# q/k from natural positions, an earlier v and convolution, a gate column with a ScalarE gate, and band-mask rows beside the head rows in 14 of 24 attention steps

## The chip, the cores and the metric

One core of one Trainium2 chip. The metric is the device time of one execution in microseconds; lower is better. Before the change three runs gave 301.47, 302.58 and 312.01 us (median 302.58). On one core the runs of one kernel scatter by 2 to 7%: a run more than 1.5% above the fastest of its kernel is called slow, and its mean granted TensorE clock is usually lower. A ratio is the mean time of one kernel's fast runs over that of the other's fast runs of the same rounds, so it is not quite the ratio of the medians quoted beside it.

## The reference, cut to what matters

```python
x = A_q                                          # [1, 2048, 640], bf16
g = sigmoid((x * gate_w).sum(-1, keepdims=True)) # one gate value per position
a = x * (causal_fft_conv(shortconv(A_k) * A_v, ssm_k) + shortconv(A_k) * A_v * ssm_D)
# b: 32 heads of 20, every query sees 8 keys, 2 positions apart
q, k, v = split(x @ B_wqkv)
b = softmax(q . k[pos - 2*w] / sqrt(20), w = 0..7) . v @ B_wo
out = g * a + (1 - g) * b
```

Of the kernel before, what the change touches and what calls it, by code (L numbers as in the profile page):

```python
# [76 lines left out]
def attn_consts():  # L77
# [21 lines left out]
    return dict(mk=_np_bf16(mkz.reshape(128, -1)), mq=_np_bf16(mqz.reshape(128, -1)), valid=_np_bf16(valid), ident=_np_bf16(np.eye(128)))  # L99
# [35 lines left out]
def kernel(  # L135
# [37 lines left out]
    xTn = p0.tile([128, NDT, 2, XP], BF, name="xTn", tag="hT")  # L173
# [10 lines left out]
    xT = pC.tile([128, NDT, XW], BF, name="xT")  # L184
    Wp = pC.tile([128, NDT, 2, NDT, 4, 32], BF, name="Wp")
    WV = pC.tile([128, NDT, D], BF, name="WV")
    wg = pC.tile([128, NDT], BF, name="wg")
    valid = pC.tile([128, 18], BF, name="valid")
    sB = ExitStack()
    pB = sB.enter_context(tc.tile_pool(name="pB", bufs=1, side="left", reuse_waits="tile"))  # L190
    wl = pB.tile([128, 4, D], BF, name="wl")
    wraw = pB.tile([128, D, 4], BF, name="wraw")
    Wn = pB.tile([128, NDT, 2, D], BF, name="Wn", tag="Wn")
# [24 lines left out]
    for c in range(4):  # L218
        load_x(c)
    nc.sync.dma_start(WV[:], W3[:, :, 2, :])  # L220
    nc.vector.memset(xTn[:, :, :, 0:PRE], 0.0)
    nc.vector.memset(xTn[:, :, :, PRE + S // 2:XP], 0.0)
    nc.gpsimd.dma_start(wraw[:], raw(A_shift_k, 0, [[0, 128], [4, D], [1, 4]]))
    nc.gpsimd.dma_start(valid[:], ca["valid"].ap())
    nc.gpsimd.dma_start(wg[:], gate_w.rearrange("(t p) -> p t", p=128))
    load_kv(0)
# [14 lines left out]
    def kv_gen():  # L241
# [3 lines left out]
        for c in range(4):  # L245
# [9 lines left out]
            kvo = pB.tile([128, 4 * D], BF, name="kvo", tag="kvo", bufs=2)  # L255
# [14 lines left out]
    def transposes(j):  # L270
        tr = ppv.tile([128, 8, 128], BF, name="trx", tag="trx")
        for dt in range(NDT):
            nc.tensor.transpose(tr[:, dt, :], xN[:, j, 128 * dt:128 * dt + 128], ident[:, :])
        a = PRE + 128 * (j // 2)
        ld.copy(xTn[:, :, j % 2, a:a + 128], tr[:, 0:NDT], NDT * 128, eng="ad"[j % 2])

    def windows(e, g):
        n = 6
        s0 = xTn[:, :, e, QB * n * g:QB * n * g + QB * (n - 1) + KB]
        src = bass.AP(tensor=s0.tensor, offset=s0.offset, ap=[list(s0.ap[0]), list(s0.ap[1]), [QB, n], [1, KB]])  # L280
        c0 = (NSB * e + n * g) * KB
        nc.vector.tensor_copy(xT[:, :, c0:c0 + n * KB].rearrange("p t (b k) -> p t b k", k=KB), src)  # L282

    def vproj(m):
        ps = ppv.tile([128, 2, 512], F32, name="psv", tag="mm", bufs=3)
        for a in range(2):
            for dt in range(NDT):
                nc.tensor.matmul(ps[:, a, 0:320], lhsT=xT[:, dt, 128 * m:128 * m + 128], rhs=WV[:, dt, 320 * a:320 * a + 320],  # L288
                                 start=(dt == 0), stop=(dt == NDT - 1))
        nc.scalar.copy(VW[:, m, :, 0:DH].rearrange("p (a h) d -> p a h d", a=2),  # L290
                       ps[:, :, 0:320].rearrange("p a (h d) -> p a h d", h=16))

# [6 lines left out]
    def gate():  # L299
        grow = pB.tile([1, S], F32, name="grow", tag="Wn")  # L300
        for c in range(6):
            gps = ppv.tile([128, 512], F32, name="gps", tag="trx")
            for dt in range(NDT):
                rhs = xT[:, dt, 384 * c:384 * c + 384].rearrange("p (b c) -> p b c", c=KB)[:, :, PRE:KB]
                nc.tensor.matmul(gps[0:1, 0:6 * QB], lhsT=wg[:, dt:dt + 1], rhs=rhs,
                                 start=(dt == 0), stop=(dt == NDT - 1))
            p = 6 * QB * (c % 3)
            n = min(6 * QB, S // 2 - p)
            nc.scalar.activation(grow[:].rearrange("o (n two) -> o two n", two=2)[:, c // 3, p:p + n], gps[0:1, 0:n], ACT.Exp, scale=-1.0)
        nc.sync.dma_start(g_scr[:].unsqueeze(0), grow[:])  # L310
        for g in range(4):
            nc.sync.dma_start(g_nat[32 * g:32 * g + 32, :], raw(g_scr[:], 16 * g, [[64, 32], [1, 16]]))
# [12 lines left out]
    def permute_w():  # L325
        for w in range(2):
            nc.scalar.copy(Wp[:, :, w, :, :, 0:DH].rearrange("p a t h d -> p a (t h) d"),
                           Wn[:, :, w, 0:400].rearrange("p a (h d) -> p a h d", d=DH))
            yield
            nc.scalar.copy(Wp[:, :, w, :, :, DH:32].rearrange("p a t h d -> p a (t h) d"),  # L330
                           Wn[:, :, w, 400:D].rearrange("p a (h d) -> p a h d", d=32 - DH))
            yield

    QKP = ((1, KB, 0, 0), (0, QB, PRE, KB))

    def qk_part(ft, c, part, ps):
        which, wd, off, z = QKP[part]
        nb = 8 if c < 4 else 4
        for dt in range(NDT):
            rhs = xT[:, dt, 512 * c:512 * c + KB * nb].rearrange("p (b c) -> p b c", c=KB)[:, :, off:off + wd]  # L340
            nc.tensor.matmul(ps[:, 0:nb * wd], lhsT=Wp[:, dt, which, ft].rearrange("p h c -> p (h c)"), rhs=rhs,  # L341
                             start=(dt == 0), stop=(dt == NDT - 1))

    def qk_evac(ft, c, part, ps, eng):
        _, wd, _, z = QKP[part]
        nb = 8 if c < 4 else 4
        ld.copy(kq[ft // 4][:, ft % 4, 8 * c:8 * c + nb, z:z + wd], ps[:, 0:nb * wd].rearrange("p (b c) -> p b c", b=nb), nb * wd, eng=eng)
# [10 lines left out]

    def qk_gen(fts):
        for ft in fts:  # L360
            for c in range(5):
# [528 lines left out]
```

## The kernel before: what the change and the argument touch

Positions are split into even and odd; 36 windows of 64 keys and 57 queries cover them. The tiles `kq` hold k and q side by side, 4 heads per tile at partitions 32h. A head has 20 rows, so partitions 32h+20 to 32h+31 are free. The q/k projection fills them with pieces of the heads 20 to 31, and `send_rest` copies these pieces by DMA to their proper places in the second `kq` tile.

```python
def send_rest(ft):                     # SP queue, 28 copies in all
    ...
        nc.sync.dma_start(kq[1][dst:dst + n, t % 4, :, :],
                          kq[ft // 4][src:src + n, ft % 4, :, :])   # n partitions x 8712 B

def scores(i):                         # half an attention step: two heads
    gi, t, hf = halves[i]
    for hh in range(2):                # band mask: a matmul of 11 rows ahead of the scores
        r = 32 * (2 * hf + hh)
        nc.tensor.matmul(sc[:, hh, 0:NW], lhsT=mk[r:r + NF, :], rhs=mq[r:r + NF, :], start=True, stop=False, ...)
    ...                                # then 24 small score matmuls, 20 rows each, added to the mask
            nc.tensor.matmul(sc[...], lhsT=kqt[r:r + DH, t % 4, si, 0:KB],
                             rhs=kqt[r:r + DH, t % 4, si, KB:CB], start=False, stop=True, ...)
    nc.scalar.activation(ETs[i % NET][...], sc[...], ACT.Exp, scale=SCALE)

# main order: all transposes, windows of x (VectorE), v, gate, q/k of two feature tiles,
# rest of the convolution, load_hn(0), load_hn(1), send_rest(0), send_rest(1), then
# 24 attention steps with "units" of later work between their parts:
# steps 0-7 q/k of three tiles, 8-11 late v, from 12 on output projection and the first FFT
```

`load_hn` loads the long filter (512 KB each) which VectorE transposes during attention; both it and the copies use the one SP queue, whose timelines show the issues in program order, each behind the waits of those ahead of it. `b_scr` is a DRAM scratch that takes the attention output from the tile `fin`. `kv_scr`, `G`, `Hb` and `qg` belong to the FFT stages and the final product.

## Time and profile before

| Profiled run of before (fast, span 302.1 us, mean clock 0.932) | starts at, us |
|---|---|
| first v matmul | 20.27 |
| first q/k matmul | 46.35 |
| first attention score | 64.80 |
| first late v matmul (step 8) | 112.49 |
| first output projection (step 12) | 134.53 |
| first `s<-Am,G` matmul (FFT stage after attention) | 187.03 |
| first load of `qg` from the SP queue | 209.71 |
| last inverse stage | 280.75 |

I call these the milestones and read them off TensorE's and the queue's timelines. A change that gains in one stage shows as an earlier milestone. The views themselves are in the prediction.

### The profile page before, as it was taken

How to read it: one execution, taken by the hardware profiler on the slowest of the kernel's cores; microseconds unless marked ns; L12 is line 12 of the kernel's file. 1: busy time of each engine (PE TensorE's matmuls, PEld its weight loads, DVE VectorE, ACT ScalarE, POOL GpSimd, SP SyncE). 2: the span in 40 equal slices, each digit the busy share in tenths (PEclk: the TensorE clock that was granted, in tenths of full speed). 3: DMA queues.
4: the chain of work that ended last, by engine and by line, in shares of the span. 5: the costliest groups of instructions: out<-in, count | busy, mean ns of one | idle time of the engine just before them, and what ended most of it. 6: DMA issues, size and time to landing. Idle time of an engine off the chain costs nothing. (4 is left out here: it accounts for less than half of the span.)

```text
span 302.1 us, 12078 instructions
## 1 busy us (share of the span) xinstructions
PE 246.1 (81%) x5468; PEld 170.3 (56%) x5482; DVE 199.8 (66%) x304; ACT 175.6 (58%) x247; POOL 17.3 (6%) x36
## 2 busy tenths in 40 slices
PE   2569959999999996999889998997968789587530
PEld 1447624554545454556556665776867769577410
DVE  2169999995248686687346465319578597975692
ACT  2344864566434452354537564789587868976670
POOL 3820000000000000000000000000000000000042
PEclk9999989999999997799999999999797969997955
DMA  7999722023665515103664242274998762360075
GB/s 223 339 311 403 282 81 85 4 89 98 152 147 131 100 46 113 57 2 98 180 184 118 86 138 89 58 162 94 243 282 207 186 139 70 75 158 2 4 208 142
DMA packets 18842, 42.19 MB, mean 140 GB/s; under 512 B 3944, under 2 KB 11448, under 8 KB 17783
## 3 DMA queue, kind: packets, MB, share of 16 engines
q1 hardware_dynamic: 17800, 39.21, 46.5%
q0 software_dynamic: 992, 2.23, 2.9%
q8 instruction: 42, 0.69, 1.0%
q14 instruction: 8, 0.07, 0.1%
HBM read 26.22 MB, written 7.87 MB: 113 GB/s over the span
## 5 line engine op out<-in xcount | busy, mean ns | idle before, releaser
L341 PE MATMUL pj<-xT,Wp 128*128 128x456 bf16 (+3 forms) x236 | 50.7, 347 | 0.9 <-issue 0.3
L587 ACT ACTIVATE ET<-sc 128x684 bf16<-128x684 f32 x48 | 34.3, 740 | 18.1 <-PE sc L584 17.5
L122 ACT CAST kq<-pj 128x456 bf16<-128x456 f32 (+3 forms) x39 | 19.5, 528 | 26.7 <-PE pj L341 26.4
L341 PEld LDWEIGHTS <-Wp 128*128 128x128 bf16 x250 | 21.7, 97 | 18.1 <-issue 0.3
L452 PE MATMUL s<-Am,G 64*128 64x64 bf16 x1280 | 22.4, 190 | 9.6 <-issue 6.2
L485 DVE TENSOR_TENSOR Hb<-Up,Hb 128x1024 bf16<-128x1024 bf16 x40 | 25.3, 687 | 7.3 <-DMA Hb<-Hb 4.4
L498 PE MATMUL i<-M,Hb 128*128 128x128 bf16 x320 | 26.6, 249 | 4.1 <-DVE Hb L485 4.0
L122 ACT CAST Am<-s 128x1024 bf16<-128x1024 f32 x27 | 26.6, 1036 | 3.8 <-PE s L428 3.5
L498 PEld LDWEIGHTS <-Hb 128*128 128x128 bf16 x320 | 25.0, 153 | 6.1 <-DVE Hb L485 5.7
L452 PEld LDWEIGHTS <-G 64*128 64x128 bf16 x1280 | 20.0, 95 | 12.7 <-issue 8.8
L648 DVE CAST fin<-op 128x320 bf16<-128x320 f32 x24 | 11.7, 489 | 19.2 <-PE op L643 17.9
L643 PE MATMUL op<-wo,oT 128*128 128x320 bf16 x120 | 20.0, 300 | 4.1 <-ACT oT L630 2.7
L247 DVE TENSOR_TENSOR pr<-kvw,wl 128x2560 bf16<-128x2560 bf16 x16 | 22.8, 1487 | 0.1
L122 ACT CAST Hb<-s 128x1024 bf16<-128x1024 f32 x19 | 19.0, 1024 | 4.5 <-PE s L452 4.5
L606 PEld LDWEIGHTS <-ET 64*64 64x64 bf16 x1152 | 13.6, 110 | 13.3 <-issue 11.9
L517 DVE STREAM_TRANSPOSE hb<-hn 128x512 bf16<-128x512 bf16 x20 | 20.0, 1045 | 0.2
L616 DVE TENSOR_TENSOR oS<-O,rd 128x240 bf16<-128x240 f32 x48 | 17.3, 403 | 3.9 <-DMA kv_scr<-kvo 3.1
L584 PE MATMUL sc<-kq 20*64 20x57 bf16 x1152 | 18.4, 192 | 0.0
L606 PE MATMUL O<-VW,ET 64*64 64x21 bf16 x1152 | 18.0, 180 | 0.1
L288 PE MATMUL psv<-WV,xT 128*128 128x320 bf16 x120 | 16.5, 299 | 1.5 <-DVE xT L282 1.5
L122 ACT CAST Cm<-i 128x1024 bf16<-128x1024 f32 x13 | 12.9, 1031 | 8.1 <-PE i L498 7.3
L584 PEld LDWEIGHTS <-kq 20*64 20x64 bf16 x1152 | 13.2, 106 | 7.5 <-issue 7.5
(74 smaller groups left out, 367.7 us busy)
## 6 DMA issues: line engine op xcount, KB each, us to landing
Hb<-Hb SPq DMA_DIRECT2D x10, 512.0 KB
xN<-in_A_q_dram SPq DMA_DIRECT2D x4, 640.0 KB
kvw<-in_A_k_dram SPq DMA_DIRECT2D x4, 640.0 KB
kv_scr<-kvo SPq DMA_DIRECT2D x4, 640.0 KB
hn<-in_A_ssm_k_dram SPq DMA_DIRECT2D x5, 512.0 KB
kv<-kv_scr SPq DMA_DIRECT2D x16, 160.0 KB
qg<-in_A_q_dram SPq DMA_DIRECT2D x16, 160.0 KB
b_scr<-fin SPq DMA_DIRECT2D x36, 60.0 KB
```

Source lines behind the costliest of these rows:

```text
L122: self.nc.scalar.copy(dst, src)
L247: nc.vector.tensor_tensor(pr[:, j].rearrange("p (n c) -> p n c", n=4), kh[:, 4 * c + 3 - j:4 * c + 7 - j, :], wl[:, j, :].unsqueeze(1).to_ ...
L341: nc.tensor.matmul(ps[:, 0:nb * wd], lhsT=Wp[:, dt, which, ft].rearrange("p h c -> p (h c)"), rhs=rhs, start=(dt == 0), stop=(dt == NDT - 1))
L452: nc.tensor.matmul(o, lhsT=G[rows, j, r, :], rhs=Am[rows, 2 * j + r, :, :], start=(r == 0), stop=(r == 1), tile_position=(64 * c, 0), skip ...
L485: nc.vector.tensor_tensor(blk_(H_), blk_(Up), blk_(H_), ALU.mult)
L498: nc.tensor.matmul(o, lhsT=src[:, c, :, :, 8 * oc + il].rearrange("p q j -> p (q j)"), rhs=M[:, k, :], start=(k == 0), stop=(k == 1), skip ...
L517: nc.vector.transpose(hT[:, g].rearrange("p (c n) i -> p n c i", c=2)[:, 16 * p:16 * p + 16], hnb[0][:, g % 2].rearrange("p (a n) -> p n a ...
L584: nc.tensor.matmul(sc[64 * sub:64 * sub + 64, hh, QB * mb:QB * mb + QB], lhsT=kqt[r:r + DH, t % 4, si, 0:KB], rhs=kqt[r:r + DH, t % 4, si, ...
L587: nc.scalar.activation(ETs[i % NET][:, :, 0:NW], sc[:, :, 0:NW], ACT.Exp, scale=SCALE)
L606: nc.tensor.matmul(O[64 * par:64 * par + 64, s, 21 * sl:21 * sl + 21], lhsT=ET[rows, hh, QB * mb:QB * mb + 64], rhs=VW[rows, NMB * gi + mb ...
L616: nc.vector.tensor_tensor(dst, Ov[:, s, :, 0:DH].rearrange("p (b h) d -> p b h d", h=4), rd[:, s].rearrange("p (b h) -> p b h", h=4).unsqu ...
L643: nc.tensor.matmul(op[:, 0:320], lhsT=oTs[j][:, ft, :], rhs=wo[:, ft, 320 * hf:320 * hf + 320], start=(ft == 0), stop=(ft == NDT - 1))
```

## The change

Its intent: start attention earlier (v as soon as part of x is there, no window copies of x for q/k, no separate gate matmuls), take the gate's scaling away from VectorE, and save the pair of mask matmuls where the free partitions of `kq` can carry the mask as 11 more contracted rows.

```diff
+    mkq = np.tile(np.concatenate([mk, mq], axis=1), (1, 36))      # DRAM constant, 11 rows x 8712 B
 ...
-    for c in range(4): load_x(c)
-    nc.sync.dma_start(WV[:], W3[:, :, 2, :])
+    load_x(0); load_x(1)
+    nc.sync.dma_start(WV[:, :, 0:D], W3[:, :, 2, :])              # column 640 of WV is gate_w
+    load_kv(0); load_x(2); load_x(3)
 ...
+    def v_win(m, pool, bufs): ...                                  # window copy for one v tile, VectorE
+    def v_gate(m, ps): nc.scalar.activation(gexp[:, m:m + 1], ps[:, 320:321], ACT.Exp, scale=-1.0)
     def gate():   # was: 30 matmuls; now: 12 stores of 4-byte elements, 4 loads
+        L_.append((raw(g_scr[:], e + 2 * QB * (2 * m0 + sub) + 2 * i, [[2, c], [4 * QB, nm]]), gexp[...]))
+        return L_ + [(g_nat[32 * g:32 * g + 32, :], raw(g_scr[:], 16 * g, [[64, 32], [1, 16]])) for g in range(4)]
 ...
-            rhs = xT[:, dt, 512 * c: ...]                          # q/k from windows, 5 chunks
+            rhs=xTn[:, dt, c // 3, a:a + n]                        # from natural positions, 6 chunks
 ...
+    def mask_rows(t, n, h):                                        # SP queue
+        nc.sync.dma_start(kq[t // 4][32 * h + DH:32 * h + DH + NF, t % 4:t % 4 + n]..., mkq rows, n times)
     def scores(i):
+        own = gi == 2 or t > 4
+        K = DH + NF if own else DH                                 # 31 rows instead of 20
+        for hh in range(0 if own else 2): (mask matmuls)
 ...
+    KC = 3                                                         # the convolution runs into steps 0-2
+    mplan = {k: [(5, 3, k - 3)] for k in range(3, 7)}              # 4 DMAs of 3 tiles, 281 KB
+    mplan.update({9 + t: [(t, 1, h) for h in range(4)] for t in range(5)})   # 20 of one tile, 94 KB
 ...
+        if k == KC - 1:                                            # end of step 2
+            new_kq(1)
+            for ft in range(...): send_rest(ft)                    # 17 copies at once
+            load_hn(0); load_hn(1)                                 # were ahead of the copies
+        for a_ in mplan.get(k, []): mask_rows(*a_)
+            paced += gl                                            # the gate's transfers, SP queue, behind G
 ...
-        for q in range(4): nc.scalar.copy(yt[..., 480 elements])
+        for tt in range(m): nc.scalar.activation(yt[... 640 elements], ACT.Copy, scale=g_nat[:, t0 + tt])
```

## The prediction

> **What bounds the kernel now.** I read the stage view first (busy time in stretches that I cut at the trace's own seams), then TensorE's timeline, then the chain of waits. Columns of the first: stretch, its length, busy time (instructions) of PE, PEld, DVE, ACT, POOL, the granted clock, DMA share, GB/s.
>
> ```profile
> 0.00:20.27 20.27, 8.25 (x80) 6.96 (x81) 5.83 (x13) 6.96 (x9) 10.47 (x19) 1.00 0.90 282
> 20.27:36.70 16.43, 16.43 (x121) 11.68 (x122) 16.26 (x14) 9.55 (x12) 0.00 (x0) 1.00 0.93 364
> 36.70:46.35 9.65, 6.37 (x31) 3.02 (x32) 9.58 (x6) 6.54 (x11) 0.00 (x0) 0.82 0.22 71
> 46.35:64.79 18.44, 18.39 (x98) 9.48 (x98) 18.23 (x13) 9.16 (x19) 0.33 (x4) 1.00 0.23 72
> 64.79:106.00 41.21, 40.16 (x872) 20.51 (x882) 24.31 (x42) 20.99 (x36) 0.00 (x0) 1.00 0.51 116
> 187.00:209.70 22.70, 21.51 (x500) 17.09 (x501) 8.71 (x12) 19.40 (x24) 0.00 (x0) 1.00 0.41 101
> 280.75:302.10 21.35, 6.16 (x512) 4.62 (x512) 12.45 (x13) 10.43 (x24) 6.00 (x12) 0.67 0.47 125
> ```
>
> The first 20 us are transfers (DMA share 0.90) with TensorE busy 8 of 20; then TensorE is the bound without a gap until 187 us, except the gate, which costs 9.65 us for 6.4 us of work. After 187 the transposed FFT stages alternate between engines and the transfer queue; the last 21 us are VectorE's.
>
> ```profile
> 5.36 1.25 PE L273 MATMUL trx<-ident,xN 128*128 128x128 bf16 x10 [5.36 <-DMA xN<-in_A_q_dram]
> 11.12 1.25 PE L273 MATMUL trx<-ident,xN 128*128 128x128 bf16 x10 [2.71 <-DMA xN<-in_A_q_dram]
> 41.43 4.76 PE L305 MATMUL gps<-xT,wg 128*1 128x342 bf16 x20 [3.12 <-ACT grow L309]
> 72.60 0.32 PE L577 MATMUL sc<-mq,mk 11*128 11x342 bf16 x2
> 72.85 0.38 PE L584 MATMUL sc<-kq 20*64 20x57 bf16 x24
> 119.05 1.49 PE L376 MATMUL pv<-WV,xT 128*128 128x320 bf16 x5 [2.14 <-DVE hb L517]
> ```
>
> Each pair of mask matmuls (L577) holds TensorE for 0.25 us, start to start, before 24 score matmuls of 0.31 us. From the chain of waits, in order of time (start, length):
>
> ```profile
> 196.33 1.42 SPq L637
> 197.80 1.77 SPq L637
> 200.62 3.30 DMA b_scr<-fin
> 204.20 0.84 DVE fin L663
> ```
>
> After attention the one transfer queue (SP) is itself on the chain: anything put in it at 185 to 195 us may come out as time.
>
> **What the Trainium skill says.** "TensorE: Matmul & The Clock Gate", section LDWEIGHTS: a weight load takes time by its columns, not its rows. The trace agrees: 11 rows by 128 columns 91 ns, 128 by 128 97 ns, 20 by 64 106 ns. So 31 contracted rows instead of 20 should be free. "ScalarE: Activation LUTs", section What ACT_TABLE_LOAD costs: about 186 ns plus 0.833 ns per element, and 93 ns more for a per-partition scale. The first half agrees (1024 elements 1036 ns here); no run here shows the second yet. "DMA: Bandwidth & Descriptors", section Anatomy of one DMA: DMA engines wait on no semaphore, the issuing sequencer does, and a transfer has about 2 us of fixed cost; the row Min transfer for line-rate of its Specifications puts that at 512 B. The trace has the fixed part (2.8 us for a 120 KB store of the output); transfers of 4-byte elements, which the new gate makes, are in no large number in it.
>
> **The change, part by part.**
>
> *Gate (out of TensorE).* 30 matmuls and the wait for ScalarE go: the whole 9.65 us stretch. In their place the v projection gets a 321st column in half of its 180 matmuls (one column more: nothing), and ScalarE 18 activations of one element, about 0.2 us each by the formula above, beside a v projection of 1.36 us with ScalarE busy 0.69: hidden.
>
> *Front.* The queue now carries x0, x1, the v weights, the first k and v chunk, then x2, x3. The bytes ahead of x3's end are 5.2 MB plus 0.64 MB of the broadcast filter; before, the same number of bytes had moved at about 19 us (the sum of the GB/s of slices of one or two us), so I put x2 at 18 to 19 us and x3 at 20. TensorE: chunk 1's transposes end near 14 us, as before (DMA 11.1 plus 3.0). Then v for four tiles, 4 x 1.36 = 5.4, to 19.5; chunk 2, whose copies are now all ScalarE's 0.71 us and follow v's last copy: 2.9, to 22.4; three v tiles 4.1, to 26.5; chunk 3 2.8, to 29.3; two and three v tiles 6.8, to 36.1. So q/k starts at 36.1, where the gate started before: the early v fills waits but the later x gives it back. Gain: 46.35 - 36.1 = 10.2 us.
>
> *q/k from natural positions.* Columns per feature tile fall from 2304+2052 to 2094+2052, 4.8%. First two tiles: 18.44 x 0.952 = 17.55, gain 0.9. Late three tiles: the timeline gives 1.18, 1.09, 0.65 and 0.59 us for 512, 456, 256 and 228 columns, that is 0.12 us plus 2.07 ns a column, so 349 and 342 columns take 0.84 and 0.83; per tile 10.32 falls to 10.02, gain 0.9. ScalarE's 24 copies, some 0.42 us each (1.04 per pair of 968 elements, less 242 x 0.83 ns), plus eight weight permutes, 5.5 us, come to 15.6 of 17.5 us: just hidden by three buffers. Attention thus starts at 53.6 instead of 64.8, 11.1 us earlier.
>
> *Convolution on VectorE.* Its work does not shrink: 1.5 + 22.8 + 11.3 + 6.0 + 6.0 = 47.6 us, gap-free from 23.5 to 71.4 before. By the order of instructions it now begins after chunk 1 (about 16 us), but stands behind windows of chunk 2 and of chunk 3 that need ScalarE's copies: waits to about 23.4 and 30.3. I work out 58.7 us for the first O normalisation and 76.6 for the convolution's end. Attention's first three steps have five q/k units each: 1.12 (scores) + 0.60 + 5 x 0.84 = 5.9 us, so step 3 begins at 72.3 and its third unit needs, at 75.1, a PSUM buffer that VectorE empties only at 77.1. Cost 2.0 us.
>
> *Mask rows.* 14 of 24 steps, 28 halves, lose a pair: 28 x 0.25 = 7.0 us. Between 144 and 187 us TensorE also waits for oT and fin, 3.8 of 43 us, so not all arrives: 6.2. The 32 row blocks of 96 KB, 3.1 MB, go into stretches with a DMA share under 0.5 several steps ahead of use: nothing.
>
> *Gate values to natural order.* Twelve stores of 4-byte elements and four loads that wait for them are new in the SP queue, eleven of the stores and the loads ahead of the last attention output stores: 11 issues at about 0.35 (as an output store), one wait of 2.5, four loads at 0.43 (1.72 for the four before), some 8 us from 187. The view of SP's waits gives the queue 6.4 us of idling on fin there, of which I count 5 as usable. Cost 3.0, on the chain lines above.
>
> *ScalarE gate.* 16 VectorE scalings of 0.38 (6.1 us) leave the inverse stages. Most lie beside waits for swaps: gain 0.8. In the end, 3 activations of 640 elements with a scale, about 0.75 each, replace 4 copies of 480 at 0.49 per group; VectorE at 2 x 1.16 per group stays the bound: cost 0.3.
>
> *The pause at 117 us.* 2.1 us idle, then matmuls at a reduced clock (1.49 against 0.85 us for a group), 4.4 in all; the trace names a VectorE instruction that had ended. Nothing in the change removes it; a moved schedule may. I count a third: gain 1.5.
>
> Sum: -11.1 - 0.9 - 6.2 + 2.0 + 3.0 - 0.8 + 0.3 - 1.5 = -15.2, so 302.6 - 15.2 = 287.4.
>
> **Rivals.** (1) VectorE becomes the bound from 58 to 77 us. For it: the convolution is 47.6 us of unbroken work and attention starts 11 us earlier, while the convolution ends 5 us later. If the windows hold it longer, each microsecond comes out in full: time 290 to 294. (2) The front arrives earlier than I think, because x2 and x3 land by 16 us: VectorE and TensorE both gain about 3, time near 284. Against it: x1 landed only at 11.12 with three transfers behind it. (3) The gate's small transfers hide entirely behind the fin waits, or not at all: 284 or 290. (4) Mask rows late: each is sent two or more steps of 5 us ahead; a late one would show as TensorE waiting on a DMA of kq. I think it unlikely; 289.
>
> **Range and chances.** The front (3 either way), the hand-over of VectorE (+5, -2), the gate's queue time (3 either way) and the pause (1.5 up, 3 down) are nearly independent: about 6 together. So 281 to 294. A gain of less than 2%, over 296.5, needs most of the front lost: 0.04 and slower 0.02.
>
> **What would show it.** Right: no gps line; pj starts near 36 and score matmuls near 54; about 40 L577-like mask matmuls instead of 96, score matmuls of 31 rows still about 190 ns; VectorE at nine tenths until about 77 us and TensorE pausing near 75 for it; SP's wait for the gate store near 190 us with fin waiting longer; yt activations of 640 near 0.75 us. Wrong: score matmuls slower with 31 rows; q/k start beyond 40 us, because transfers came later; TensorE waiting on kq rows; ScalarE full in the q/k stretch.

## The result, and the profile after

The changed kernel is correct and slower: 335.5 us median of four runs (332.04 to 342.86) against 307.29 us for before on the same chip in the same rounds (301.47 to 322.64). The ratio of the fast runs is 1.098, 95% interval 1.080 to 1.116. The profiled run is slow (span 335.4 us, clock 0.858).

| Milestone, us | before | after | difference |
|---|---|---|---|
| first v | 20.27 | 12.63 | -7.6 |
| first q/k | 46.35 | 35.74 | -10.6 |
| first score | 64.80 | 53.50 | -11.3 |
| first late v | 112.49 | 128.65 | +16.2 |
| first output projection | 134.53 | 148.19 | +13.7 |
| first `s<-Am,G` | 187.03 | 208.90 | +21.9 |
| first `qg` load | 209.71 | 239.64 | +29.9 |
| last inverse stage | 280.75 | 312.08 | +31.3 |
| end | 302.1 | 335.4 | +33.3 |

The front came out as predicted. Then 27.5 us are lost between the first score and the first late v, 8.2 in the output projection, 8.1 between the FFT stage and the `qg` load, and 2.0 in the last stage. The stage view of after, columns as in the prediction (stretch, length, PE, PEld, DVE, ACT, POOL, clock, DMA share, GB/s):

```profile
20.24:35.74 15.50, 13.78 (x120) 10.23 (x121) 9.49 (x10) 11.54 (x26) 0.00 (x0) 1.00 0.96 376
35.74:53.50 17.76, 17.76 (x122) 11.54 (x120) 17.55 (x12) 14.46 (x32) 0.26 (x4) 1.00 0.26 75
98.90:128.20 29.30, 2.75 (x50) 1.37 (x38) 6.58 (x12) 1.19 (x2) 0.00 (x0) 0.58 0.59 85
158.00:180.00 22.00, 14.16 (x264) 8.79 (x264) 11.34 (x21) 5.47 (x8) 0.00 (x0) 0.61 0.72 161
210.00:240.00 30.00, 22.36 (x462) 17.18 (x460) 9.35 (x15) 19.16 (x22) 0.00 (x0) 0.89 0.34 73
```

The third line holds most of the loss: in 29.3 us TensorE works 2.75. DMA engines are busy 0.59 of the time and move only 85 GB/s, where the front moved 376 at 0.96. So the engines are occupied for far longer per byte than before. TensorE's timeline of after says what it waited for (start, length, group, in brackets the idle time before it and what ended it):

```profile
106.32 1.58 PE L350 MATMUL pj<-xTn,Wp 128*128 128x342 bf16 x5 [7.30 <-DVE kq L125]
112.88 0.25 PE L600 MATMUL sc<-kq 31*64 31x57 bf16 x1 [4.97 <-DMA kq<-ca_mkq]
122.16 0.53 PE L600 MATMUL sc<-kq 31*64 31x57 bf16 x23 [9.03 <-DMA kq<-ca_mkq]
125.94 0.25 PE L600 MATMUL sc<-kq 31*64 31x57 bf16 x1 [3.25 <-DMA kq<-ca_mkq]
128.18 0.54 PE L600 MATMUL sc<-kq 31*64 31x57 bf16 x23 [1.99 <-DMA kq<-ca_mkq]
```

Four waits, 19.2 us, are for mask rows (`ca_mkq`). The first one, 7.3 us, is for a VectorE copy out of PSUM. That is only the visible end of a chain; VectorE's timeline shows that it stood behind a wait for the filter:

```profile
103.68 0.16 DVE L531 TENSOR_TENSOR hn<-hn,D 128x1 bf16<-128x1 bf16 x1 [8.78 <-DMA hn<-in_A_ssm_k_dram]
```

And the SP queue shows why the filter was late. First the queue of before, then that of after (start, time taken by the issues, DMA, number):

```profile
71.97 2.02 SPq L511 DMA_DIRECT2D hn<-in_A_ssm_k_dram  x2
74.09 13.13 SPq L356 DMA_DIRECT2D kq<-kq  x11
```

```profile
77.51 14.21 SPq L364 DMA_DIRECT2D kq<-kq  x17
91.77 1.79 SPq L527 DMA_DIRECT2D hn<-in_A_ssm_k_dram  x2
...
103.58 9.55 SPq L368 DMA_DIRECT2D kq<-ca_mkq  x3
```

Before, the two filter loads go first; after, they stand behind 17 head copies and are issued 20 us later: 14.2 us for the copies, 5.5 because the stores of the convolution, ahead of both, end later (77.4 against 71.9). Three mask-row DMAs hold the queue for 9.55 us. At the end of attention the gate's stores do the same on a smaller scale: the queue of after, then VectorE of after waiting for an output store that is behind them:

```profile
207.71 0.42 SPq L668 DMA_DIRECT2D g_scr<-gexp  x1
...
213.13 3.03 SPq L783 DMA_DIRECT2D g_scr<-gexp  x8
220.35 1.89 SPq L783 DMA_DIRECT2D g_nat<-g_scr  x4
222.28 3.13 SPq L653 DMA_DIRECT2D b_scr<-fin  x8
```

```profile
225.14 0.82 DVE L679 CAST fin<-op 128x640 bf16<-128x640 f32 x1 [10.17 <-DMA b_scr<-fin]
```

In total that wait of VectorE is 17.2 us after, 5.4 before.

### The profile page after: what moved, and what is told of

Same layout as the page of the kernel before. It is cut to its first block, busy times and chain, and to the rows that moved or that the text cites. A ratio compares the mean times of both kernels' runs of the same rounds, so it can differ in the third digit from the quotient of the medians.

```text
span 335.4 us, 12066 instructions
## 1 busy us (share of the span) xinstructions
PE 240.0 (72%) x5446; PEld 174.1 (52%) x5446; DVE 198.3 (59%) x298; ACT 177.6 (53%) x271; POOL 17.3 (5%) x36
## 5 line engine op out<-in xcount | busy, mean ns | idle before, releaser
L350 PE MATMUL pj<-xTn,Wp 128*128 128x349 bf16 (+1 forms) x300 | 50.5, 314 | 8.1 <-DVE kq L125 7.9
L350 PEld LDWEIGHTS <-Wp 128*128 128x128 bf16 x300 | 26.9, 98 | 21.2 <-issue 8.1
L468 PE MATMUL s<-Am,G 64*128 64x64 bf16 x1280 | 25.6, 199 | 16.9 <-issue 6.5
L123 ACT CAST kq<-pj 128x342 bf16<-128x342 f32 (+1 forms) x50 | 22.1, 471 | 27.4 <-PE pj L350 26.9
L468 PEld LDWEIGHTS <-G 64*128 64x128 bf16 x1280 | 23.0, 101 | 20.5 <-issue 16.4
L600 PE MATMUL sc<-kq 31*64 31x57 bf16 (+1 forms) x1152 | 18.5, 199 | 19.6 <-DMA kq<-ca_mkq 19.2
L659 PE MATMUL op<-wo,oT 128*128 128x320 bf16 x120 | 23.2, 334 | 10.5 <-DVE fin L664 5.2
L600 PEld LDWEIGHTS <-kq 31*64 31x64 bf16 (+1 forms) x1152 | 13.7, 111 | 28.6 <-issue 16.6
L123 ACT CAST Am<-s 128x1024 bf16<-128x1024 f32 x22 | 22.0, 1034 | 10.5 <-PE s L444 10.5
L514 PEld LDWEIGHTS <-Hb 128*128 128x128 bf16 x320 | 22.7, 150 | 6.4 <-DVE Hb L501 5.7
L664 DVE CAST fin<-op 128x320 bf16<-128x320 f32 x24 | 11.6, 487 | 21.9 <-PE op L659 10.3
L293 PEld LDWEIGHTS <-vw 128*128 128x128 bf16 x180 | 17.5, 103 | 8.6 <-issue 1.2
L659 PEld LDWEIGHTS <-oT 128*128 128x128 bf16 x120 | 11.7, 105 | 15.6 <-issue 8.8
```

Of the source, the lines that this page charges most:

```text
L123: self.nc.scalar.copy(dst, src)
L293: nc.tensor.matmul(ps[:, 0:320 + a], lhsT=vw[:, dt].rearrange("p b k -> p (b k)"), rhs=WV[:, dt, 320 * a:320 * a + 320 + a], start=(dt == ...
L350: nc.tensor.matmul(ps[:, 0:n], lhsT=Wp[:, dt, which, ft].rearrange("p h c -> p (h c)"), rhs=xTn[:, dt, c // 3, a:a + n], start=(dt == 0), ...
L468: nc.tensor.matmul(o, lhsT=G[rows, j, r, :], rhs=Am[rows, 2 * j + r, :, :], start=(r == 0), stop=(r == 1), tile_position=(64 * c, 0), skip ...
L514: nc.tensor.matmul(o, lhsT=src[:, c, :, :, 8 * oc + il].rearrange("p q j -> p (q j)"), rhs=M[:, k, :], start=(k == 0), stop=(k == 1), skip ...
L600: nc.tensor.matmul(sc[64 * sub:64 * sub + 64, hh, QB * mb:QB * mb + QB], lhsT=kqt[r:r + K, t % 4, si, 0:KB], rhs=kqt[r:r + K, t % 4, si, K ...
```

## The experiments

Eighteen kernels ran, in six calls; those of a call share the runs of before. A "lead" is how much earlier a milestone comes than in the profiled run of before. The profiled runs of seven kernels carry the label slow (no mask rows; no rows with gate from GpSimd and the filter behind; mask rows alone; rows unread; v bursts; held back; held back with v bursts).

### Call 1: what of the change costs, taken out of after

**No mask rows.**

```diff
-        own = gi == 2 or t > 4
+        own = False
-    mplan = {k: ...}; mplan.update(...)
+    mplan = {}
```

> The changed kernel with its band mask as before: mask matmuls in all 24 steps, no mask row transfer. Theory M (the mask row transfers are what attention waits for at 99 to 128 us and again at 155 to 180): both losses go, the mask matmuls come back with 7 us, the front's 11 us stay won and the gate stores' 8 us stay lost: 298 to 304 us. Theory Q (the copies of the remaining heads and the hn loads alone are already too late, because attention now overtakes them by 11 us): TensorE still stands for 10 us or more before step 9, 308 to 316 us.

**Gate's transfers from GpSimd's queue.**

```diff
-            paced += gl
+            for p_ in gl: nc.gpsimd.dma_start(*p_)
```

> The changed kernel with the twelve gate stores and four gate loads on the Pool queue, right when the last gate column is there, in place of the SP queue. Theory G (these sixteen transfers hold the SP queue from 208 to 222 us and with it the output stores of attention): the stretch from the last attention step to the first q load falls from 31 us to about 23, the run is 7 to 9 us faster than the changed kernel (323 to 326). Rival (that stretch is slow for another reason, the swaps or the clock): within 2 us of the changed kernel.

**Mask rows only for the third group of queries, a third of the bytes.**

```diff
-        own = gi == 2 or t > 4
+        own = gi == 2                       # and only blocks 24 to 35 of each row are written
```

> Mask rows used in the last eight steps only, and only the 12 of 36 blocks that these read are sent: 32 row blocks of 32 KB instead of 96, all of them from step 9 on. Theory M: TensorE no longer stands before step 9 on mask rows; 16 of the 28 removed mask pairs stay removed (4 us): 294 to 301 us. Theory Q: as for the version without mask rows, less 3 us, 305 to 313.

**Mask rows from GpSimd's queue.**

```diff
-        nc.sync.dma_start(kq[...mask rows...])
+        nc.gpsimd.dma_start(kq[...mask rows...])
```

> The changed kernel with the same mask rows, full length, sent from the Pool queue instead of SP. If what costs is the order in the one SP queue (mask rows behind the head copies and hn loads, and these behind mask rows): 305 to 315 us. If what costs is the time of the DMA engines on single-partition rows of 8.7 KB, on whatever queue: 322 to 335 us.

| Run | median (range), us | ratio of fast runs |
|---|---|---|
| no mask rows | 312.52 (308.96 to 319.26) | 1.028 [1.014, 1.043] |
| gate from GpSimd | 333.38 (324.34 to 336.69) | none given |
| third group, sliced | 319.03 (318.23 to 319.82) | 1.054 [1.046, 1.061] |
| mask rows from GpSimd | 329.72 (327.62 to 331.37) | 1.088 [1.078, 1.099] |

Without the mask rows some 20 us come back (1.098 falls to 1.028), so they are the largest part. They are not all: that kernel still waits 8.33 us on VectorE for the filter, leads by only 1.1 us at the first late v, and ends slower than before. A third of the bytes for 8 of 24 steps still costs 2.5% over no rows. GpSimd's queue for the rows helps little (329.7): the 17 head copies on SP took 19.4 us there instead of 14.2, so the two queues meet again at the DMA engines. Gate stores off SP: the stretch from the first `s<-Am,G` to the first `qg` load falls from 30.7 to 24.0 us (before 22.7), so the gate's queue time is about 7 us, not 3. Against the expectations: no mask rows ended in theory Q's range; the sliced rows, at 319, outside both ranges; the rows from GpSimd where the theory of engine time put them; and of the gate's run only the stretch followed theory G, for its median is 2 us under after's and a single run of it (324.34) counts as fast.

### Call 2: mask rows alone on the old kernel, and the filter's place

**Mask rows alone, on before** (the three hunks of the rows: constant, `mask_rows` and `mplan`, `own` in `scores`; nothing else).

> The kernel before with nothing but the mask rows of the change (14 of 24 steps, same sends at the same steps). My prediction's step said minus 6.2 us: 296. Theory C (the rows cost transfer time in themselves: 3.1 MB to 11 partitions each, 8.7 KB a row, about 3.1 us per 281 KB and 1.0 us or more per 94 KB, in a queue with head copies): TensorE waits on DMA of the mask rows for 5 us or more in steps 8 to 11 and the output stores are late, total 306 to 318. Theory R (the rows are late only because the new front lets attention overtake the transfers): no waits on them here, total 294 to 299.

Measured: 324.79 us median (321.37 to 326.86), ratio 1.068 [1.053, 1.082]. The rows cost 20 us without any overtaking front: theory C, and more than it said. Two lines of TensorE's waits in that run (us in total, times, longest):

```profile
PE sc L591 <- DMA kq<-ca_mkq: 8.1, 2, 5.1
...
PE O L613 <- issue: 6.8, 2, 5.4
```

Only 8.1 us are waits for the rows themselves. 6.8 us are put down to nothing the profile shows ("issue"), in the middle of a group, while the queue issues twelve mask-row DMAs. The first late v comes 9.3 us late and the first `s<-Am,G` 23.2.

**Filter loads ahead of the head copies; all else as after.**

```diff
             new_kq(1)
+            load_hn(0); load_hn(1)
             for ft in range(...): send_rest(ft)
-            load_hn(0); load_hn(1)
```

> After, with only the hn loads ahead of the head copies; mask rows and gate as in after. Theory T: the 8.8 us wait of VectorE for hn near 95 us goes and TensorE's idle stretch of 7.3 us before 106 with it, but the mask rows then are simply waited for earlier: they need about 29 us of transfer in the queue after the head copies, so TensorE still idles 12 to 19 us on kq rows before 128, total 328 to 336, within 2% of after. Rival V (the hn loads' place is the cause and the rest follows from it): total under 318.

Measured: 329.41 us median, ratio 1.090 [1.079, 1.102]. The 7.3 us wait is gone and the first late v comes at 118.4 instead of 128.7. But TensorE still waits for mask rows four times (3.89, 7.35, 3.23, 2.59 us), and it ends within 2% of after, as theory T said. The filter's place is real and second to the rows.

**No mask rows, gate from GpSimd, with and without the filter first.**

> After, without the mask rows (every step takes its mask matmuls), with the gate's stores and loads issued from GpSimd's queue, and with the two hn loads ahead of the 17 head copies instead of behind them. Theory T (transfer queue and engines: the front's gain is real, and it is lost to three things put in the transfer path: mask rows, the place of the hn loads, the gate's stores): VectorE's wait for hn (8.3 us in the run without mask rows) falls under 1 us, first late-v matmul near 104 to 106 us instead of 111.35 (before: 112.49), s2 to first qg load about 23 us instead of 33, total 288 to 294, some 3 to 5% faster than before. Rival U (the front's lead is paid back anyway, because attention then waits for the late q/k units or VectorE): late v near 110, total 300 to 304, same as before.

> As the first of this call, but with the hn loads left behind the head copies. The difference between the two is what that wait costs alone. Theory T: VectorE waits about 8 us for hn at 96, late v near 111, total 296 to 302 (7 us more than the first of this call). Rival U: no difference over 2 us.

Measured: filter first 311.37 us (308.17 to 324.38), ratio 1.028; filter behind 312.18 (306.78 to 315.78), ratio 1.024. The waits moved as theory T said: VectorE's 8.23 us wait for `hn` is gone with the filter first, late v comes at 106.2 against 110.1, and the stretch to the `qg` load is 24 us in both. The total did not move: theory T fell on its number. TensorE is not waiting in the filter-first kernel; it is slow. Its stage view:

```profile
94.00:104.00 10.00, 10.00 (x211) 5.43 (x208) 5.61 (x13) 3.94 (x7) 0.00 (x0) 0.83 0.63 96
106.00:116.00 10.00, 9.82 (x175) 5.29 (x176) 6.12 (x14) 2.46 (x6) 0.00 (x0) 0.59 0.45 89
116.00:126.00 10.00, 10.00 (x173) 5.12 (x172) 6.74 (x15) 3.21 (x8) 0.00 (x0) 0.50 0.19 54
126.00:136.00 10.00, 10.00 (x154) 5.35 (x153) 4.64 (x8) 3.78 (x8) 3.60 (x6) 0.50 0.10 5
136.00:146.00 10.00, 9.02 (x148) 5.00 (x148) 5.00 (x11) 2.77 (x4) 2.00 (x4) 0.50 0.57 118
```

Busy 10.00 of 10.00 with a clock of 0.50: a full row of the busy view, and less work done. (The 0.83 of the first line is a shorter stretch of half clock, 3.4 us from 94.1, after a pause of 1.17 us.) The long one begins 1.6 us after the end of this pause:

```profile
106.18 0.85 PE L293 MATMUL pv<-WV,vw 128*128 128x320 bf16 x5 [1.62 <-DVE vw L287]
```

To compare kernels I summed, over slices of 2 us, TensorE's busy time times (1 - granted clock). Call it the clock loss; it is an estimate from the view, beside the idle time of the same stretch.

| Profiled run, 90 to 160 us | idle, us | clock loss, us |
|---|---|---|
| before | 5.8 | 2.7 |
| after | 32.0 | 4.3 |
| no mask rows | 11.1 | 7.1 |
| no rows, gate from GpSimd | 12.7 | 16.6 |
| the same, filter first | 5.0 | 21.7 |

The filter-first kernel idles no more than before, and loses 19 us more by the clock. This is not a matter of slow runs: its three fast runs have mean clocks of 0.861 to 0.890, the four of before in these rounds 0.942 to 0.946.

### Call 3: traffic or waits; the pause or the load

**Rows written but not read, on before** (mask rows alone with `own = False`: the transfers stay, the mask matmuls stay).

> The kernel before; the mask rows are written as in the run of mask rows alone (same transfers, same steps, same places), but no matmul reads them: the steps keep their mask matmuls of 11 rows and the scores read 20 rows. So TensorE can wait for no mask row; only the traffic is left. Mask rows alone cost 22 us over before, of which the trace shows 8.1 us as TensorE waiting for the rows themselves. Theory W (the cost is the wait for the rows and what the clock loses after it): time 300 to 305, same as before. Theory Tr (the rows' transfers hold the DMA engines and the queue, and what stands behind them is late: head copies, hn, output stores, instruction fetch, seen as 'issue' stalls of TensorE of 5.4 us in the middle of a group at 139): 312 to 322, with 'issue' stalls of several us near 140 and fin waits of 4 us and more at 155 to 175.

Measured: 327.03 us median (321.13 to 331.43); its two fast runs, 321.13 and 324.61, stand against one fast run of before in these rounds, 298.86. So no ratio is given, but the sense is plain and agrees with the run of mask rows alone: unread rows cost as much as read ones. The waits are now for what shares the transfer path with the rows, here the head copies:

```profile
127.14 0.38 PE L591 MATMUL sc<-kq 20*64 20x57 bf16 x23 [1.91 <-DMA kq<-kq]
129.43 0.22 PE L591 MATMUL sc<-kq 20*64 20x57 bf16 x1 [1.66 <-DMA kq<-kq]
```

The stall near 140 that I expected did not come (one of 2.1 us came at 115), and part of the loss was again clock (16.8 us of clock loss between 160 and 210). The sense of theory Tr holds, its detail did not.

**Window copy of v tile 12 made after step 5** (on the filter-first kernel; this removes the 1.62 us pause).

```diff
     def late_v():
         nxt = v_win(12, pC, 2)
+        yield
 ...
+        if k == 5: advance(fg["v"], 1)
```

> The first kernel of the last call (no mask rows, hn loads first, gate stores from GpSimd; 309.8 us in the profile) with one more move: the window copy of v tile 12 is made after step 5 instead of in step 8, where TensorE waited 1.6 us for it at 106 us and then ran at half clock until 148 (TensorE busy 56 of 60 us there, mean clock near 0.6, loss by clock 21.7 us between 90 and 160 against 2.7 in before). Theory K (the pause starts the half clock, and the loss is only that): no pause near 105, clock near 1.0 to 150, total 290 to 296. Rival K2 (the clock's fall comes from the load itself or from any small gap, so that another pause starts it): clock low somewhere else in 90 to 160, total 300 to 312.

Measured: 305.98 us median (303.49 to 307.26), all four fast; no ratio, since before had one fast run (298.86). The stage view:

```profile
106.00:116.00 10.00, 9.15 (x257) 5.57 (x251) 9.86 (x21) 5.37 (x12) 0.00 (x0) 1.00 0.49 114
116.00:126.00 10.00, 9.17 (x248) 5.75 (x251) 7.57 (x15) 4.14 (x9) 3.61 (x6) 1.00 0.24 34
126.00:136.00 10.00, 4.42 (x95) 2.85 (x94) 3.91 (x9) 2.79 (x5) 2.01 (x4) 0.81 0.58 136
136.00:146.00 10.00, 9.60 (x168) 5.27 (x168) 5.47 (x11) 2.90 (x5) 0.00 (x0) 0.50 0.49 144
```

Both theories get a half. With the pause gone, the clock is 1.00 where it was 0.50 and the first output projection comes at 121.0, a lead of 13.6 us: the front's gain is real, and larger than at the start. Then another pause, 5.24 us for a `fin` buffer, starts half clock again, for 31 us, and the `s<-Am,G` milestone is 1.6 us behind before.

**Late v in one run of 15 matmuls per step** (on the filter-first kernel, pause kept).

```diff
+        if 8 <= k < 12: cut = [0, 0, 3, 3, 3]
```

> The same kernel (no early window copy) with the three late v units of each of steps 8 to 11 issued in one run of 15 matmuls of 128 by 128 by 320 instead of one per quarter step. The pause at 106 stays. Theory D (at half clock a mix of v units of 1.5 us and 24-fold groups of 57 or 21 columns does not release the clock; 4.5 us of full-size matmuls in one piece does): clock back at 1.0 by 115 instead of 148, total 292 to 300. Rival D2 (it comes back by chance or by something else): half clock for over 20 us again, 303 or more.

Measured: 308.25 us median (301.40 to 309.99). After the same pause (1.61 us) the clock was back by about 106, so D seemed right; but half clock came three more times (3.4, 17.1 and 13.7 us; the second with a `fin` wait of 3.6 us), and no run of the four reached 300.

### Call 4: shape or bytes; which transfer stands in the way

**Same bytes, wide, on before** (24 of the 32 row blocks, those up to step 11, to a spare tile of 128 partitions by 748 B), and **the same 24 blocks to their 11 partitions**; nothing reads either.

```diff
-        nc.sync.dma_start(kq[t // 4][32 * h + DH:32 * h + DH + NF, ...], mkq rows)   # 11 x 8712 B
+        nc.sync.dma_start(mdb[:, h, 0:n], raw(mkq, 0, [[374, 128], [0, n], [1, 374]])) # 128 x 748 B
```

> The kernel before, with 24 of the 32 mask-row blocks (those up to step 11) written not to 11 partitions of 8712 B but, with the same bytes, to a spare tile of 128 partitions by 748 B; nothing reads it. Theory Sh (shape: rows of 11 partitions keep 11 DMA engines for long, and what stands behind them is late): same as before, 299 to 305, and the first output projection matmul within 2 us of before's 134.5. Theory By (the bytes, 2.2 MB more in the stretch): like the next run.

> The kernel before, with the same 24 blocks written to their 11 partitions as in the change, unread. Under both theories late: first output projection matmul 4 to 9 us after before's 134.5 (with all 32 it was 141.6), total 308 to 325.

Measured: wide 308.81 us (305.73 to 309.20), ratio 1.024 [1.009, 1.038]; narrow 316.53 (310.80 to 331.43), ratio 1.040 [1.000, 1.081]. The intervals overlap, so the total alone does not settle it; the milestone that I had named does. First output projection: wide 134.29, narrow 141.70, before 134.53. The stretch of 101 to 121 us, the narrow run first and then the wide one:

```profile
101.00:121.00 20.00, 12.29 (x303) 6.46 (x302) 11.44 (x21) 5.47 (x9) 0.00 (x0) 0.85 0.63 92
```

```profile
101.00:121.00 20.00, 18.89 (x455) 10.28 (x452) 14.07 (x27) 7.71 (x13) 0.00 (x0) 0.91 0.66 130
```

At nearly the same DMA share the wide form moves 130 GB/s and TensorE works 18.89 us of 20; the narrow form moves 92 and TensorE works 12.29. Shape rather than bytes makes the delay at step 12, in one profiled run of each, both fast. The totals do not divide so clearly: by the means of the fast runs the wide form costs about 7 us over before and the narrow one about 12, so the same bytes in a good shape still cost something; 1.8 us of it is in the front of the wide run's profile (first score 66.61 against 64.80).

The page "DMA: Bandwidth & Descriptors" of the Trainium skill, section "Why a DMA increments its semaphore by 16 and not by 1", says that a DMA runs on the largest number up to 16 of engines that divides the slowest dimension of both sides, and from the SP queue on the lowest-numbered ones. That gives 11 engines for 11 partitions and 4, 8 or 12 for the head copies, all out of the same low numbers, and 16 for 128 partitions. The runs agree in what it leads to (0.59 share with 85 GB/s in after). No view shows the single engines, but the packet records in the traces can be counted: at 112 to 116 us of after, where rows of 8712 bytes are nearly all that moves, 11 packets are in flight 70% of the time; at 105 to 109 us of the wide run there are 15 on average. That rows from GpSimd's queue slowed the copies on SP too (19.4 against 14.2 us) is measured; which engines they had there is not.

The largest wait in the narrow run stands in the middle of a score group:

```profile
121.27 0.37 PE L591 MATMUL sc<-kq 20*64 20x57 bf16 x11 [7.97 <-issue]
```

"issue" means that the profile shows nothing it waited for. Six head copies in the queue took 8.8 us at that time, 4.3 in the wide run. The DMA records point to something else: the fetch of TensorE's own instructions. The DMA view has a queue of kind "instruction" (q8, packets of 16 KB; 42 of them in before, for 10950 matmuls and weight loads). In the wide run its packets start at 104.3, 112.5 and 117.5 us; in the narrow run at 102.9 and then not before 117.8. That packet landed at 119.7, and TensorE went on 1.5 us later. Over all twenty traces, between 50 and 215 us, TensorE has 22 waits of 0.8 us or more with the releaser "issue"; 19 of them end 1.3 to 1.8 us after such a landing, among them all eight above 2.05 us. Landings are 5.7 us apart in the median, so by chance some two would. Late instructions are thus the likely cause of these waits; no run was made to test it.

**Gate's stores in step 17, and besides that the later filter loads from GpSimd** (both on the early-window kernel).

```diff
-    (in step 12)     for p_ in gl: nc.gpsimd.dma_start(*p_)
+    if k == 17:      for p_ in gl: nc.gpsimd.dma_start(*p_)
+    load_hn: (nc.sync if g < 2 else nc.gpsimd).dma_start(...)     # second kernel only
```

> The last kernel (early window copy; 304.5 us, clock 1.0 to 130, then 5.2 us of TensorE waiting for fin, half clock from 134 to 164) with the gate's stores and loads issued from GpSimd in step 17 instead of step 12, where the DMA share was 0.3 to 0.5 at 6 to 30 GB/s just before the wait. Theory G (the 4-byte stores kept hn's last load and so the fin stores late): no fin wait over 2 us near 130, clock 1.0 to 150 or later, time 288 to 296. Rival (hn's last load and the kv loads in the queue ahead of the fin stores do it anyway): fin wait of 3 us or more near 130, half clock after it, 300 to 306.

> The same, and the last three hn loads (512 KB each) issued from GpSimd's queue, so that none stands in SP's queue ahead of fin stores waiting for a buffer. If hn in the queue is the cause of the fin wait, it is gone here: 288 to 294. If neither the gate nor hn is, 300 to 306, with the wait at the same place.

Measured: 309.96 us (306.05 to 319.93), ratio 1.018 [0.994, 1.042]; and 306.16 (302.62 to 310.17), ratio 1.013 [0.993, 1.034]. The first edit did nothing: GpSimd's queue has its own order and nothing to wait for, so the stores still went out at 122 us. The `fin` wait was 4.62 us there and 1.82 in the second, and half clock followed both. In the second, the DMA engines were busy at 0.77 with 23 GB/s (134 to 136 us). I took that for the 4-byte stores, but the DMA view puts 76.9% on ten packets of the SP queue and 0.2% on GpSimd's queue, which has the stores; why those ten packets, of 5120 bytes, took 2.1 to 3.3 us each is not shown.

### Calls 5 and 6: the stores held back, with and without bursts

**Gate stores held back by a dependency on step 18; filter transposes from step 4; filter loads three to five from GpSimd.**

```diff
+        if k == 18:
+            nc.gpsimd.tensor_copy(gexp[:, 19:20], ETs[(2 * k) % NET][:, 0, 0:1])
+            for p_ in gl: nc.gpsimd.dma_start(*p_)
-        if k > KC + 2: advance(ht, 2)
+        if k > KC: advance(ht, 2)
```

> New front, no mask rows, hn loads first (two from SP, three from GpSimd), hn transposes from step 4 instead of 6, early window copy, gate stores and loads from GpSimd held back by a dependency on step 18's probabilities. Theory G2 (4-byte stores and hn's last load are what delays fin): no TensorE wait for fin over 1.5 us between 120 and 160; loss by clock in 90 to 160 under 6 us instead of 12; first s2 matmul at 178 to 183 (before 187), total 290 to 298. Rival (head copies and kv loads are enough to stop TensorE, or the clock falls anyway): half clock for 20 us or more in 110 to 165, total 300 to 306.

**The same with all units from step 8 on in one run per step** (`cut = [0, 0, n, n, n]` for k >= 8).

> The same, and from step 8 on all late v, output projection and FFT units of a step in one run after its second score group. Theory D (long runs of full-size matmuls release the clock soon; seen once, 4 us at 103 where the spread mix took 40): every half-clock stretch in 90 to 190 under 12 us, loss by clock in 90 to 210 under 5 us, total 286 to 296. Rival D2 (chance): stretches of 20 us or more remain. Cost of the burst in waits for oT, fin and PSUM buffers 2 to 5 us either way.

**The same with bursts for late v alone**, five rounds.

> The kernel with held-back gate stores (303.2 us in its profile, a slow one; 297.9 its best; before in the same rounds 304 to 324), with the three late v units of each of steps 8 to 11 in one run. If long runs of full-size matmuls release the clock: half clock after the pause near 105 lasts under 10 us instead of 20, first output projection matmul near 126 to 128 instead of 132.0, total 294 to 300, and some 2% faster than before. If the return is chance: half clock of 15 us or more there, and 300 to 306, same as before.

| Run | median (range), us | ratio of fast runs |
|---|---|---|
| held back | 304.69 (297.93 to 307.17) | none given |
| held back, all bursts | 315.10 (314.44 to 320.84) | 1.033 [1.027, 1.039] |
| held back, v bursts | 304.00 (299.32 to 310.43) | 0.998 [0.988, 1.008] |

The stores now go out from 157 us on and no `fin` wait above 0.8 us is left before 160: theory G2 is right about the waits, and the total is the rival's. But another pause came (3.40 us at 105, "issue"), and half clock for 20 us after it. All bursts lose: a 4.36 us wait for a head copy, waits for `fin` and `oT`, and half clock for 14 us and later for 20. The last run goes against theory D. Its fast runs, 299.32 to 302.46 us, are not the 2% faster that D asked for, and their mean clock is 0.913 to 0.927 against 0.937 to 0.957 for those of before. Its profiled run (a slow one) shows, after a pause of 2.31 us, with late v in runs of 15:

```profile
106.00:116.00 10.00, 10.00 (x160) 6.00 (x161) 5.54 (x11) 3.83 (x8) 0.33 (x1) 0.59 0.71 105
116.00:126.00 10.00, 10.00 (x220) 5.84 (x218) 6.63 (x14) 3.43 (x8) 0.58 (x1) 0.50 0.19 54
```

Half clock lasted 20 us there although TensorE was busy throughout. Without mask rows and with these repairs the new front equals the old kernel and doesn't beat it: 0.998, from four fast runs of eight against six of eleven.

What sets the length of half clock? The pauses and the half clock that began in them or just after, from the profiled runs:

| Pause of TensorE | half clock, us |
|---|---|
| 2.14 us, before | 6.8 |
| 7.97 us, narrow rows | 10.2, of which 3.9 after the pause |
| 1.61 us, late v in bursts | 3.4 |
| 1.62 us, filter first | 41.0 |
| 5.24 us, early window | 30.7 |
| 2.31 us, held back, v bursts | 20.5 |

Neither the length of the pause nor, by the last and third rows, long runs of full-size matmuls alone explains it. The page "TensorE: Matmul & The Clock Gate" of the Trainium skill, section "Part 1: The HAM clock gate", has the half clock come after an idle window of about 3.4 us and go after a busy one of about 3.4 us. Here a pause of 1.6 us was enough, and twenty to forty busy microseconds were not.

The clock records of the traces narrow it down. In all twenty, every recorded stretch of half clock but the one that runs to the end of the trace lasts a whole number of 3.41 us, so the window itself is there (6.8 is two of them, 41.0 twelve). I cut each trace at these steps and added up, per window, the array work of its matmuls: moving columns, times the used share of the 128 rows, times that of the 128 columns. A v matmul of 128 by 128 by 320 counts 320 for its 300 ns; a score matmul of 20 by 64 by 57 counts 4.5 for its 192 ns. Of the 969 windows between 50 and 215 us, all 171 under 2600 are followed by a window at half clock, and all 648 over 3400 by one at full clock; between these it goes either way. With a limit of 2800 the next window's clock comes out right in 933 of 969, with the best limit on busy time in 834. The twelve windows of half clock in the filter-first kernel hold 2100 to 3100, although all but one are busy for 92% or more; the early-window kernel holds 3300 to 4400 at that place while its clock is full. So the clock goes with the work in a window, and small matmuls keep TensorE busy without doing much of it. This is a fit to these traces, made afterwards; no run was designed to test it.

## Why the prediction was wrong, point by point

- **Front: right.** q/k started at 35.74 (predicted 36.1) and scores at 53.50 (53.6). Within it some misses cancel: v began at 12.6, not near 14, its first four tiles took 6.6 us, not 5.4, and TensorE waited for x2 until 20.2, not 18 to 19. TensorE's units of late q/k took 0.84 and 0.83 us as computed.
- **Convolution: right in kind, smaller in size.** TensorE waited 0.60 us at 77.55, where I had 2.0 at 75.1.
- **Mask rows: the step that failed.** "The 32 row blocks of 96 KB, 3.1 MB, go into stretches with a DMA share under 0.5 several steps ahead of use: nothing", and rival 4, "I think it unlikely; 289". The saving on TensorE was put at 6.2 us and is not to be seen: read or unread, the rows cost about 20 us on the old kernel. I had counted bytes against a mean share. What the runs show instead: the transfers alone cost it, whether or not TensorE reads the rows; in 11 partitions they delay step 12 by 7 us, in 128 partitions by none; and the head copies beside them are late. That all of it is engine time lost to the shape is argued, since the wide form cost about 7 us in the total as well. The contracted rows themselves were nearly free, as I had said (203 ns a score matmul of 31 rows, 192 for 20). Of the weight loads, the prediction's figures show that rows hardly matter (91 ns for 11, 97 for 128), but not that columns set the time, for 64 columns took 106 ns.
- **A step that was missing: the filter loads.** The diff moves them from ahead of the head copies to behind 17 of them; I listed what moved and passed over it. In after it is a wait of 8.8 us on VectorE, seen on TensorE as 7.3. In the totals it doesn't show: with the filter first 1.090 against 1.098, and without rows 1.028 against 1.024.
- **Gate transfers: a term of the right kind, mis-sized.** I had 3.0 us; the stretch to the `qg` load grew by 8.0, of which 6.7 left when the stores left the queue. In a total of fast runs I can't show it: the two kernels without rows that differ in the gate alone stand at 1.028 and 1.024. (The 2 us of fixed cost that the prediction names are given for GpSimd's path, and the 120 KB store beside them is GpSimd's; for SP's queue I had only assumed them.)
- **The ScalarE gate: two terms off, in sum near nothing.** Three activations of 640 took 0.796 us each, 2.39 a group, so ScalarE, not VectorE (2 x 1.16), paces the last stage. By the formula in "ScalarE: Activation LUTs" of the Trainium skill, section What ACT_TABLE_LOAD costs, 640 elements with a per-partition scale are 0.81 us; the measurement agrees, and the prediction's 0.75 didn't follow the formula that it cites. With 0.81 its own sum would have put ScalarE at 2.44 and ahead of VectorE: VectorE waits 4.9 us there for `yt` against 3.1, and the stage is 2.0 us longer where I had 0.3. The inverse stages ahead of it, without the scalings, took 66.2 us with held-back stores and 67.2 with the early window against 69.3, where I had 0.8; in after itself, at its lower clock, 70.5.
- **The pause at 117: wrong sign.** I counted on 1.5 us from it vanishing. The changed schedule made more pauses, and in most repaired kernels they cost more by the half clock after them than by themselves (a clock loss of 10 to 22 us between 90 and 160, against 2.7 before).
- **The sum and the range.** I had the four sources of error together at about 6 us. None of them was the one that came: the range was built around terms I had named, and the largest risk sat in the term set to zero.

## What to carry to other kernels

Price a DMA by the engine time of its shape too, not only by bytes against a mean share: here rows of 11 partitions kept 11 packets in flight at 92 GB/s, and what was sent beside them came late. When a change moves DMA issues within one queue, list for each consumer what now stands ahead of its transfer. And a gain on TensorE lasts only if no new pause follows: look at the granted clock beside the busy time, because a fully busy stretch at half clock looks healthy in every other view; here small matmuls kept TensorE busy and did too little to bring the clock back.

## What the Trainium skill lacked or had wrong

- "TensorE: Matmul & The Clock Gate", Part 1: half clock after about 3.4 us idle, released after about 3.4 us busy. Runs here: pauses of 1.62 and 2.14 us were followed by it, and it stayed 20 to 41 us with TensorE busy for 90 to 100% of each 10 us (10.00 of 10.00 us at 0.50), while after a pause of 7.97 us it ended within 4. The 3.41 us window is confirmed. What the page lacks is a measure of activity (elsewhere it speaks of small idles that are enough, without a size): here the array work per window tells the cases apart in 933 of 969 windows, busy time in 834.
- "DMA: Bandwidth & Descriptors", the section on the semaphore's 16: the rule for the number of engines is there, and elsewhere on the page the advice to put a multiple of 16 outermost, but no figure for what narrow transfers cost each other. Here 11-partition rows of 8.7 KB moved 92 GB/s at a share of 0.63 where the same bytes over 128 partitions moved 130 at 0.66, and 17 copies of 4 to 12 partitions took 19.4 us to issue beside rows from another queue instead of 14.2.
- The same page has no figure for stores of 4-byte elements as used here: twelve of them and their four loads made the stretch that they stand in 6.7 us longer on SP's queue; from GpSimd's they took 6.6 to 7.9 us from issue to landing for 1.7 KB or less each.
- "Runtime: NRT & Kernel Launch", Instruction fetch mechanics, lacks a case in which other DMA traffic makes the fetch late. Here 19 of 22 unexplained waits, up to 7.97 us, ended 1.3 to 1.8 us after a packet of the instruction queue landed (likely, not tested).
